# How entry 0's x is fetched at the start of a spectral filter with a SoLU block behind it: rows, transfers and queues

## The chip, the cores and the metric

The kernel runs on one core of a Trainium2 chip. The metric is the device time of one execution in microseconds (us); runs are summed up by their median. The engines are TensorE (PE; its weight loads are listed apart as PEld), VectorE (DVE), ScalarE (ACT), GpSimd (POOL) and SyncE (SP). SP, ScalarE and GpSimd can issue DMA transfers, each through a queue of its own; 16 DMA engines carry them.

## The reference

Eight entries of 3136 rows and 256 channels are filtered in the frequency domain along the rows; the 25088 rows that come out go through a block with two matrix products and a softmax-weighted activation between them. All is fp32.

```python
X = np.fft.rfft(x, axis=1)                     # x: 8 x 3136 x 256
y = np.fft.irfft(X * (filt_r + 1j * filt_i)[None], n=3136, axis=1)
h = y.reshape(25088, 256) @ w_in               # 256 x 1024
sm = softmax(h)
solu = h * sm
ln = (solu - mean(solu)) / sqrt(var(solu) + 1e-6) * g_ln
out = ln @ w_out                               # 1024 x 256
```

## The kernel before, in words

**The transform.** 3136 is 49 x 64 (`N1`, `N2`). A row number is 64 * n1 + n2. The kernel takes n2 together with 63 - n2: on the partitions, "half 0" holds the 49 values of n1 for n2 = 0 to 31 (partitions 0 to 48) and "half 1" the 49 values for n2 = 63 down to 32 (partitions 49 to 97), so half 1 is read mirrored, with a negative step. `rows_x` is the tile of entry 0: 98 partitions by 32 (`NH`) columns by 256 channels, a column being one value of n2. It is loaded in 8 pieces of 4 columns (`NCH`) for each half. In HBM, 4 columns of one n1 are 4 KB in a row, and the next n1 is 64 KB further.

**The opening**, entry 0, is in this order by engine:

- SP issues the table `wf_t` (L540), then half 0 of x (L535): piece 0 as 48 rows, then the 49th row of all 32 columns as one transfer of 32 KB, then pieces 1 to 7 as 48 rows each. After that come the stores of pa's last 4 rows.
- ScalarE's queue issues the table `one` (L541).
- GpSimd issues half 1 of x, 8 mirrored pieces of 49 rows (L535), with two blocks of `w_in` between them (`begin`, L425), then the tables and filter rows of the first four pairs of residues (`load_tables(0, 4)`, L481 and L484: one `de`, eight `f`), then those of the next four.
- TensorE runs `first` (L238, "pa") on each piece: two products of 98 x 100 by 98 x 512. ScalarE copies the result over x (L240) and stores it to the DRAM scratch `d1`: 96 rows from ScalarE's queue (L193), the other 4 from SP's (L194).
- TensorE then runs five products without use (`idle_row(5, "idle")`, L563), which read `de` and `f`, so they wait for all loads of `load_tables(0, 4)`.
- SP fetches `d1` back with frequencies on the partitions (`t`, then into spare places of `y`; L303). TensorE runs `forward` (L313, "pb"), VectorE and GpSimd multiply by the filter (L334 to L336), TensorE goes back (L313, "pc"), and ScalarE copies and stores `g` to the scratch `d2` (L351, L355).
- 14 more products without use ("idler", L563) stand before the last step of entry 0 (L409, "py"), which reads `d2` through SP's fetches (L363). SP then fetches half of entry 1's x (L476).
- Between these, VectorE, ScalarE and GpSimd turn the weights, which arrive as 64-bit numbers, into fp32 (`convert`).

**The rest.** From about 100 us on a loop over blocks of 128 rows (`step`) runs both matrix products, the activation and the transforms of the entries that follow; the changed code doesn't touch it.

The order of the work is written by hand (`tc.manual_schedule()`): each engine runs its instructions in the order in which the code emits them. The waits are derived from the tiles that are read and written. A DMA transfer tells of its landing by counting up a semaphore; there are eight such semaphores for the queues of SP and ScalarE together, used in turn, and eight for GpSimd's. The ninth transfer therefore takes the semaphore of the first, and where nothing else has ensured that the first has landed, the issuing engine waits for it.

## Time and profile before

| what | us |
|---|---|
| median of three runs | 1596.14 (1591.15 to 1606.48) |
| profiled execution | 1601.33 |
| its span | 1599.6 |
| TensorE's mean granted clock in it | 0.994 |

The profile is of one execution, so sums are made against its own 1601.33 us. The span runs from the first to the last instruction. The opening's other rows, from the timeline and the DMA view (queue, transfers, size of each):

| what | count and size |
|---|---|
| half 0 of x, SP | 8 of 192 KB and 1 of 32 KB |
| half 1 of x, GpSimd | 8 of 196 KB |
| raw blocks of `w_in` before the filters, GpSimd | 2 of 512 KB |
| `f` of the first eight pairs, GpSimd | 16 of 128 KB |
| stores of pa, ScalarE and SP | 8 of 384 KB and 8 of 16 KB |

pa's first product starts at 10.58 us and the last ends at 26.78; the eight copies of pa take 1.01 us each, the first at 14.35, the last at 28.07. The first filter product of VectorE (L334) starts at 43.30. How the profile is read: a line of the timeline or the chain gives a start and a length; an engine's "idle before" is put down to whatever released it last; and an idle engine off the chain costs nothing.

### The profile page before, as it was taken

What the parts mean: (1) busy time and instruction counts of PE and PEld (TensorE: products, weight loads), DVE (VectorE), ACT (ScalarE), POOL (GpSimd) and SP (SyncE); (2) the same over time, 40 slices, a digit from 0 to 9 for tenths busy, and PEclk for the clock granted to TensorE, in tenths of its full rate; (3) what the DMA queues carried; (4) which work ended last, traced back from release to release, by engine and by line L of the source; (5) the groups of instructions that cost most, each with busy time, mean ns of one, the idle gap of its engine ahead of it and who ended that gap; (6) DMA issues with size and microseconds to landing.
All of it is one profiled execution on the core that took longest, in us unless ns stands there. A gap on an engine that the chain in (4) does not pass through costs nothing.

```text
span 1599.6 us, 36769 instructions
## 1 busy us (share of the span) xinstructions
PE 1551.8 (97%) x12828; PEld 1058.8 (66%) x12828; DVE 1250.7 (78%) x2248; ACT 921.4 (58%) x1874; POOL 1169.7 (73%) x1371
## 2 busy tenths in 40 slices
PE   5998999999999999999999999999999999999997
PEld 1463566666666676677666677667766777777777
DVE  1887878897987788876988789887888777777673
ACT  2246555656665656666565655666565656666663
POOL 5546886789677868796779867797766766676765
PEclk8999999999999999999999999999999999999999
DMA  9989878786987589766886679766784444343434
GB/s 266 290 282 269 247 215 236 215 217 181 255 241 222 155 229 256 211 183 178 221 231 202 166 193 251 204 189 179 215 224 132 126 133 122 103 113 94 116 105 116
DMA packets 343802, 311.13 MB, mean 195 GB/s; under 512 B 27834, under 2 KB 310099, under 8 KB 343619
## 3 DMA queue, kind: packets, MB, share of 16 engines
q1 hardware_dynamic: 271476, 170.45, 40.6%
q0 software_dynamic: 33744, 98.81, 21.0%
q10 hardware_dynamic: 38400, 39.53, 8.2%
q8 instruction: 104, 1.70, 0.5%
q14 instruction: 78, 0.64, 0.1%
HBM read 124.51 MB, written 81.40 MB: 129 GB/s over the span
## 4 chain that ended last, share of the span: by engine, by line
PE 84%; DMA 9%; DVE 2%; POOL 1%; issue 1%; SPq 1%; ACT 0%; DVEq 0%; POOLq 0%; ACTq 0%
PE m L759 35%; PE o L895 34%; DMA solu_t<-turn 4%; PE py L386 4%; PE pc L313 3%; PE pb L313 3%; PE pa L281 2%; DMA x<-in_x_dram 2%; DMA f<-in_filt_r_dram 1%; SPq L840 1%; PE idler L563 1%; PE pa L238 1%; PE py L409 1%; DMA out_dram<-ot 1%; POOL u L738 1%
## 5 line engine op out<-in xcount | busy, mean ns | idle before, releaser
L895 PEld LDWEIGHTS o<-w_out_sb,solu_t 128*128 128x128 f32 x3136 | 381.5, 192 | 50.2 <-issue 43.6
L895 PE MATMUL o<-w_out_sb,solu_t 128*128 128x128 f32 x3136 | 400.9, 276 | 3.6 <-DVE ot L915 2.9
L759 PE MATMUL m<-w_in_sb,s 128*128 128x512 f32 x784 | 399.0, 610 | 2.7 <-ACT h L769 1.8
L895 PEld LDWEIGHTS o<-w_out_sb,u 128*128 128x128 f32 x2352 | 307.1, 192 | 138.9 <-issue 106.0
L895 PE MATMUL o<-w_out_sb,u 128*128 128x128 f32 x2352 | 310.6, 275 | 2.5 <-POOL u L738 1.8
L759 PE MATMUL m<-w_in_sb,y 128*128 128x512 f32 x588 | 307.6, 606 | 1.5 <-DVE h L780 1.1
L805 DVE SCALAR_TENSOR_TENSOR h<-e,h 128x1024 f32<-128x1024 f32 x196 | 304.1, 1551 | 0.1
L769 ACT COPY h<-m 128x512 f32<-128x512 f32 x294 | 173.2, 589 | 206.5 <-PE m L759 187.0
L911 ACT ACTIVATE ot<-o,rs_t 128x128 f32<-128x128 f32 x392 | 143.6, 368 | 245.2 <-PE o L895 243.8
L738 POOL TENSOR_TENSOR u<-solu_t 128x512 f32<-128x512 f32 x98 | 135.5, 1383 | 195.6 <-DMA solu_t<-turn 133.6
L783 DVE CUSTOM_DVE_ANT_0 h<-m,h 128x512 f32<-128x512 f32 x196 | 134.2, 685 | 176.8 <-ACT h L769 103.0
L813 ACT ACTIVATE h<-h,nmu 128x1024 f32<-128x1024 f32 x196 | 225.0, 1148 | 52.0 <-DVE turn L823 51.8
L823 DVE STREAM_TRANSPOSE turn<-h 128x1024 f32<-128x1024 f32 x196 | 243.1, 1240 | 3.2
L793 ACT ACTIVATE e<-h,nmax 128x1024 f32<-128x1024 f32 x196 | 225.4, 1150 | 7.9 <-DVE h L805 6.5
L738 POOL TENSOR_TENSOR u<-solu_t,u 128x512 f32<-128x512 f32 x98 | 137.7, 1405 | 95.8 <-PE o L895 95.5
L759 PEld LDWEIGHTS m<-w_in_sb,s 128*128 128x128 f32 x784 | 128.1, 191 | 89.5 <-issue 68.9
L915 DVE SCALAR_TENSOR_TENSOR ot<-o,rs_t,ot 128x128 f32<-128x128 f32 x299 | 103.7, 347 | 98.8 <-ACT ot L911 59.0
L738 POOL TENSOR_TENSOR u<-u,solu_t 128x512 f32<-128x512 f32 x98 | 159.1, 1624 | 15.5 <-PE o L895 6.4
L759 PEld LDWEIGHTS m<-w_in_sb,y 128*128 128x128 f32 x588 | 96.6, 191 | 96.7 <-issue 46.6
L738 POOL TENSOR_TENSOR solu_t<-solu_t,solu_t 128x512 f32<-128x512 f32 x98 | 153.9, 1571 | 0.9
L738 POOL TENSOR_TENSOR s<-y 128x128 f32<-128x128 f32 x196 | 99.8, 509 | 0.5
L386 PEld LDWEIGHTS py<-wb_t,t 50*64 50x64 f32 x3584 | 57.6, 134 | 42.9 <-issue 18.7
(126 smaller groups left out, 1969.1 us busy)
## 6 DMA issues: line engine op xcount, KB each, us to landing
solu_t<-turn SPq DMA_DIRECT2D x780, 128.0 KB
out_dram<-ot SPq DMA_DIRECT2D x196, 128.0 KB
t<-d POOLq DMA_DIRECT2D x112, 200.0 KB, 7.0
d<-x POOLq DMA_DIRECT2D x100, 200.0 KB, 5.3
f<-f_dram POOLq DMA_DIRECT2D x39, 512.0 KB, 8.1
t<-d ACTq DMA_DIRECT2D x37, 512.0 KB
d<-g POOLq DMA_DIRECT2D x36, 512.0 KB, 5.1
x<-in_x_dram SPq DMA_DIRECT2D x112, 98.0 KB
```

Source lines behind the costliest of these rows:

```text
L386: nc.tensor.matmul(out=views[g][64 * h:64 * h + 64, cb, i, :], lhsT=t4[rows, i, c0:c0 + 64], rhs=wb_t[rows, 0:N1], start=True, stop=True)
L738: nc.gpsimd.tensor_tensor(out=out, in0=in0, in1=in1, op=op)
L759: nc.tensor.matmul(out=ms[j, bank], lhsT=lhsT, rhs=w_in_sb[:, w, :], start=m in (1, 2, 7), stop=True, skip_group_check=True)
L769: nc.scalar.copy(out=h_half(k, i), in_=ms[j, 0])
L783: nc.vector.tensor_tensor_reduce(out=h_half(k, i), in0=ms[j, bank], in1=h_half(*kept), scale=1.0, scalar=sofar, op0=ALU.add, op1=ALU.min, ...
L793: nc.scalar.activation(out=e, in_=hs[k], func=AFT.Exp, bias=nmaxs.pop(k)[:, 1:2], scale=-1.0, accum_out=esums[g][:, i:i + 1])
L805: nc.vector.scalar_tensor_tensor(out=solu, in0=e, scalar=SHRINK, in1=solu, op0=ALU.mult, op1=ALU.mult, accum_out=nmu)
L813: nc.scalar.activation(out=solu, in_=solu, func=AFT.Square, bias=nmu, scale=-float(DFF), accum_out=variances[g][:, i:i + 1])
L823: nc.vector.transpose(out=turns[g][:, :, i, :], in_=solus[k].rearrange("p (f j) -> p f j", j=32))
L895: nc.tensor.matmul(out=pos[p, bank], lhsT=lhs[:, f, :], rhs=w[:, f, :], start=f == 0 and (m in (1, 2, 7) or alone), stop=True, skip_group_ ...
L911: nc.scalar.activation(out=out_half(p, *to)[0], in_=pos[p, 0], func=AFT.Copy, scale=rs)
L915: nc.vector.scalar_tensor_tensor(out=ot, in0=pos[p, bank], scalar=rs, in1=out_half(p, *kept)[0], op0=ALU.mult, op1=ALU.add)
```

## The change

Both halves of x are fetched as 48 rows for a piece. The two 49th rows (one of each half) come in four transfers, each with every second column, 16 columns of 1 KB: two from SP, two from ScalarE's queue. The first mirrored piece is issued by ScalarE in place of GpSimd; the other seven stay with GpSimd. In the changed file the lines after L538 stand 8 to 10 further on.

```diff
+        def fetch_last_rows(h, odd, dma):
+
+            row, first = N1 * h + N1 - 1, odd if h == 0 else N2 - NH + 1 - odd
+            places = slice(odd, NH, 2) if h == 0 else slice(NH - 2 + odd, None, -2)
+            dma(out=rows_x[row:row + 1, places],
+                in_=bass.AP(tensor=x.tensor, offset=x[0].offset + ((N1 - 1) * N2 + first) * C,
+                            ap=[[N2 * C, 1], [2 * C, NH // 2], [1, C]]))
+
         st.enter_context(tc.manual_schedule())
         nc.sync.dma_start(out=wf_t, in_=wf_dram)
         nc.scalar.dma_start(out=one, in_=one_dram)
         pieces = NH // NCH
 
         fetch_x(0, 0, NCH, 0, N1 - 1, nc.sync.dma_start)
-        fetch_x(0, 0, NH, N1 - 1, 1, nc.sync.dma_start)
-        for i in range(pieces):
-            if i:
-                fetch_x(0, NCH * i, NCH, 0, N1 - 1, nc.sync.dma_start)
-            fetch_x(1, NCH * i, NCH, 0, N1, nc.gpsimd.dma_start)
+        fetch_x(1, 0, NCH, 0, N1 - 1, nc.scalar.dma_start)
+        for odd in range(2):
+            for h in range(2):
+                fetch_last_rows(h, odd, (nc.sync, nc.scalar)[h].dma_start)
+        for i in range(1, pieces):
+            fetch_x(0, NCH * i, NCH, 0, N1 - 1, nc.sync.dma_start)
+            fetch_x(1, NCH * i, NCH, 0, N1 - 1, nc.gpsimd.dma_start)
             if i in (4, 7):
                 begin(i // 7)
         load_tables(0, 4, nc.gpsimd.dma_start)
```

`fetch_x(h, n0, n, r0, rows, dma)` loads `rows` rows from row `r0` on and `n` columns from `n0` on of half `h`.

Compared with before, the program's instructions on VectorE and TensorE are the same; in the opening SP issues one transfer more, ScalarE three more and GpSimd one fewer; from pa's stores on, the order on every engine is the one of before.

## The prediction

> **What bounds the kernel now.** I read the page first, to see how large the opening is against the rest; then the chain of waits in order of time over the first 150 us; then the waits and the timeline of the opening; then busy times by stretches of 5 us.

> The page's header, its first table and its chain by engine:

> ```profile
> span 1599.6 us, 36769 instructions
> PE 1551.8 (97%) x12828; PEld 1058.8 (66%) x12828; DVE 1250.7 (78%) x2248; ACT 921.4 (58%) x1874; POOL 1169.7 (73%) x1371
> PE 84%; DMA 9%; DVE 2%; POOL 1%; issue 1%; SPq 1%; ACT 0%; DVEq 0%; POOLq 0%; ACTq 0%
> ```

> TensorE is busy 97% of the span, so 47.8 us without a matmul are all that exists outside its work, and the change touches only the first loads. The chain in order of time (start, length, what) shows what the loads gate:

> ```profile
> 3.15 12.68 DMA x<-in_x_dram
> ...
> 16.87 12.21 DMA f<-in_filt_r_dram
> ...
> 30.26 4.98 DMA f<-in_filt_r_dram
> 35.24 2.04 PE idle L563 x2
> ...
> 42.15 1.04 PE pb L313 x16
> ...
> 69.39 12.21 PE idler L563 x28
> 81.61 11.31 PE py L409 x102
> 92.92 8.22 DMA y<-in_x_dram
> ```

> The reader should see that TensorE's first transform (pa) is not on the chain at all: x loads, then GpSimd's filter loads, then the five idle products, then pb. From pb on, the chain is mostly TensorE work in a fixed order, so what reaches pb's start reaches the end unless a later transfer is not moved with it. The timeline (start, length, engine, line, what, idle before it and its releaser) gives the places:

> ```profile
> 1.22 5.43 SPq L535 DMA_DIRECT2D x<-in_x_dram  x9
> 1.38 3.98 POOL L535 DMA_DIRECT2D x<-in_x_dram  x5 [0.93 <-POOLq L1161]
> 10.58 16.19 PE L238 MATMUL pa<-x,wf_t 98*100 98x512 f32 x32 [10.58 <-DMA x<-in_x_dram]
> 10.82 0.74 POOL L535 DMA_DIRECT2D x<-in_x_dram  x1 [3.38 <-DMA x<-in_x_dram]
> 35.23 6.93 PE L563 MATMUL idle<-f,de 128*128 128x512 f32 x10 [8.45 <-DMA f<-in_filt_r_dram]
> 36.56 0.40 SPq L303 DMA_DIRECT2D t<-d  x1
> 42.08 0.66 PEld L313 LDWEIGHTS pb<-t,de 64*64 64x64 f32 x16 [0.76 <-PE idle L563]
> ```

> TensorE waits twice: 10.58 us for the first x, 8.45 us for the filters. pb is released by the idle products (42.08), not by t. The stretches of 5 us (stretch, length, busy time and count of PE, PEld, DVE, ACT, POOL, then clock, DMA share, GB/s) show that transfers fill the opening:

> ```profile
> 5.00:10.00 5.00, 0.00 (x0) 0.00 (x0) 0.00 (x0) 0.00 (x0) 2.44 (x4) 1.00 1.04 222
> 15.00:20.00 5.00, 5.00 (x13) 2.03 (x12) 0.00 (x0) 2.45 (x4) 1.88 (x3) 1.00 1.03 213
> 25.00:30.00 5.00, 1.77 (x5) 0.40 (x3) 3.07 (x7) 2.25 (x3) 2.08 (x4) 0.87 1.03 415
> 30.00:35.00 5.00, 0.00 (x0) 0.00 (x0) 0.69 (x1) 0.99 (x2) 3.58 (x7) 0.50 0.96 321
> ```

> The last column but one is the DMA share: about 1 throughout. The bytes before pb do not change, so a new order alone buys nothing; what can be bought is uneven loading of the 16 DMA engines. The completion counts that the trace keeps (16 for a transfer) show it. The first mirrored piece has 15 counts by 6.97 us and the last at 10.54; the later mirrored pieces end 12.34, 15.83, 16.57 and so on to 24.23, the last count 0.8 to 2.8 us behind the fifteenth; the filter loads after them inherit it (29.08 against 26.01). One DMA engine is some 3 us in arrears until about 33 us. Where this comes from: the 49th row of half 0 is one packet of 32 KB, on one engine, started at 3.85 and 1.93 us long; a 4 KB packet of x takes 0.28 to 0.31 us on average. The other suspect is 49 rows over 16 engines, at least 4 packets somewhere against 3 for 48 rows: 0.3 us more for a piece, 2.4 us over eight.

> **The change, part by part.**

> *The 32 KB row goes (SP issues one fewer), four transfers of 16 columns come, two from SP, two from ScalarE.* Issue costs 0.27 to 0.47 us each in SP's x rows and 0.31 to 0.38 in ScalarE's. On ScalarE three issues (the moved piece's too) make 1.1 us, done by 2.3 us; its next work is the table load at 10.59. Without that cover they would cost 1.1 us. On SP one more issue is 0.3 us ahead of pieces 1 to 7, hidden below. If the 16 columns go to 16 DMA engines, each carries 1 KB a transfer, 4 KB in all: 0.05 us a packet by the 1 KB packets of t (46 ns), so 0.2 us against the 1.93 us packet. By the rows shown, a transfer uses a number of engines that divides its rows: 98 rows 14, 96 rows 16, 49 rows 7, 4 rows 4, the one row 1 (the rest of the 16 counts come at issue: 15 at 2.18, the last at 6.32). Read by rows alone the new transfers would sit on one engine, 64 KB of it, 3.9 us at 1.93 for 32 KB, worse than before. I take 16, as the pattern that the instruction carries is 1 x 16 x 256 and its first size above one is 16. [...]

> *Three small transfers more.* Each occupies its queue for its issue only: SP's first pieces are issued 0.3 to 0.5 us apart while earlier ones are in flight, and land at most 2.9 us apart. Cost on the path 0, bounds 0 and 0.6 us (the slowest small landing behind piece 0). [...]

> *The first mirrored piece goes from GpSimd to ScalarE's queue, with 48 rows, and the other seven become 48.* GpSimd saves one issue of 0.75 to 1.0 us; its eighth x issue no longer waits 3.38 us; its next issues, the second raw block and de, still wait for pieces 1 and 2. The first matmul then waits for piece 0 of half 0 (landed 4.92), the mirrored piece (fifteenth count 6.97 while it ran on GpSimd's queue) and the small rows. I put it at 6.5, bounds 5.5 and 10.6: 4.1 us earlier. None of that is on the path by itself; it moves the copies and stores of pa.

> *A new wait.* In the changed order each transfer of SP and ScalarE waits for the one eight before it. So SP's pieces 1 to 4, free before (issued 2.04 to 3.32), now wait for the two tables (2.6 to 2.8), then piece 0 of each half (about 5 and 6); pieces 5 to 7 for the small rows. Behind them on SP stand only the 4-row stores, which need copies from 14.35 on. Their readers are pa 1 to 7. Pieces 1 and 2 with the rest of piece 0 are 9 packets an engine, 2.6 us at 0.29 alone and more with two queues beside them, which covers the 2.1 us between 2.8 and 4.9. Cost 0; uncovered, up to 1 us on pa 3.

> *The end of x.* The last mirrored piece goes from 24.23 to its fifteenth count, 21.43, or a little earlier: pa ends near 24.0 in place of 26.78. Between 10.58 and 15 us matmuls run at about half speed (0.85 us apart, then 0.43); starting early, that happens while pieces are still arriving, so it costs nothing.

> *pb's two gates.* First the filters: the last of entry 0's eight loads was issued at 28.28, on a count of 27.99 whose fifteenth was 25.21, and landed 34.92, fifteenth 34.01. So it gains between 0.9 (own laggard) and 2.8 us (issue too); one transfer fewer ahead (196 KB, 0.9 us at 222 GB/s) supports the upper half: 2.0. The idle products take 6.93 us because the granted clock is 0.5 until 38.97; if that moment stays, half of what is gained before it is lost, if it moves along nothing is: 1.0 to 2.0, I take 1.5. Second t: the last store landed 36.54, fifteenth count 34.56, its fetch was issued 36.56 and t landed 41.31, 0.8 us before it was needed. It gains 2.0 with 0.8 of slack, so it does not take over. pb starts at 40.6.

> *After pb.* The 14 idler products (12.2 us), py and the second entry's x follow on TensorE; SP's t fetches (74.74 on), which wait for the last g store (74.99), move with pb. The first t4 piece lands 78.43, 3.0 us ahead of py at 81.44. I pass the 1.5 us through whole.

> Sum: profiled execution 1601.33 (span 1599.6 and 1.7 around it) - 1.5 = 1599.8. That execution lies 5.2 above the median 1596.14 of the three runs; on the median, **1594.6**.

> **Rivals.**

> 1. *Filters later, slower.* The stores of pa (400 KB each) start about 4 us sooner and compete with the filter loads between 10 and 30 us. In 25 to 30 us, with stores, 415 GB/s were moved, but by the packet records GpSimd's queue had only 113 to 145 of it, against 230 alone (14 to 18 us). Three stores moved ahead of the filters are 1.2 MB, 2.9 us at 415. It decides once the last filter lands after 34.92; net of the 1 to 2 us won, 1 to 2.5 us slower: 1598. For: DMA share near 1. Against: loads and stores move more bytes together than loads alone, and the issue of the filters is paced by the x pieces.
> 2. *It doesn't do what it says:* the four small transfers use one engine each, the same one. The arrears stay, pa's start is near 8, pb's at 42 to 43: 1596.5.
> 3. *More than forecast:* filters and stores both gain the full 3 us and the clock rises with them, plus 1 us from fewer uneven packets: 4 us, 1592.

> **How the numbers follow.** Forecast 0.58, filters later 0.18, one engine 0.14, more 0.10. All are under 0.3% of the time, so the range is made by the scatter: the runs shown reach from 1591.15 to 1606.48, 0.96%, which is why 1% is about what a measurement here can tell from no change. Low end 1591.15 - 4 = 1587; high end the profiled 1601.33 + 2.5 = 1604. Only scatter could put it beyond 1%: 0.04 on either side, 0.92 between.

> **What would show it.** Right: first pa matmul at 5.5 to 8 us; the mirrored pieces' last counts within 1 us of their fifteenth; pa's end near 24; idle products from 33; pb near 40.6; py near 80; all later work the same length. Wrong: new small rows landing after 8 us (rival 2), the idle products starting after 35.2 although pa starts early (rival 1), or pb's gain gone by py.

## The result and the profile after

| | before | after |
|---|---|---|
| median, us (20 runs each, side by side) | 1600.03 (1589.99 to 1607.03) | 1593.63 (1588.38 to 1601.52) |
| profiled execution, us | 1601.33 | 1593.74 |
| its span | 1599.6 | 1592.0 |

The ratio is 0.9963 with a 95% interval of 0.9945 to 0.9982: 5.9 us faster, at least 2.9 and at most 8.8. Before's median in this comparison is 3.9 us above that of its first three runs, so the ratio, not the medians' distance from the forecast, is what counts.

Page of after, header and first table:

```profile
span 1592.0 us, 36774 instructions
PE 1549.7 (97%) x12828; PEld 1060.1 (67%) x12828; DVE 1249.5 (78%) x2248; ACT 921.2 (58%) x1874; POOL 1169.2 (73%) x1370
```

TensorE's busy time fell by 2.1 us and its time without a matmul from 47.8 to 42.3. The opening of after is read from its timeline (start, length, engine, line, what, idle before it and its releaser; L543 issues the small rows, the four new transfers of 16 columns):

```profile
1.72 1.54 ACTq L543 DMA_DIRECT2D x<-in_x_dram  x2
1.73 1.26 SPq L543 DMA_DIRECT2D x<-in_x_dram  x2
...
9.01 17.22 PE L238 MATMUL pa<-x,wf_t 98*100 98x512 f32 x32 [9.01 <-DMA x<-in_x_dram]
...
27.62 0.31 ACTq L193 DMA_DIRECT2D d<-x  x1
...
28.99 6.77 PE L573 MATMUL idle<-f,de 128*128 128x512 f32 x10 [2.77 <-DMA f<-in_filt_i_dram]
...
35.25 0.40 SPq L303 DMA_DIRECT2D t<-d  x1
...
39.08 1.69 PE L313 MATMUL pb<-t,de 64*64 64x256 f32 x16 [3.32 <-DMA t<-d]
40.70 2.08 PE L497 MATMUL back<-one,de 128*128 128x128 f32 x8
42.71 1.17 PE L313 MATMUL pb<-y,de 64*64 64x256 f32 x16
```

The filters release the idle products at 28.99 in place of 35.23, 6.2 us earlier. pb starts only 3.0 earlier (39.08 against 42.08): t now comes last. pb waits 3.3 us for it, where before pb followed the idle products at once. pb works in units, each on one fetched tile (t, then y): a line "pb ... x16" is one unit. Its second unit starts 3.63 us after the first; before they were 2.14 apart (42.08, 44.22). The stretches say why (stretch, length, busy time and count of PE, PEld, DVE, ACT, POOL, granted clock, DMA share, GB/s):

```profile
35.00:38.00 3.00, 0.76 (x2) 0.00 (x0) 0.00 (x0) 0.00 (x0) 1.82 (x2) 1.00 0.45 126
38.00:41.00 3.00, 1.92 (x17) 1.14 (x18) 0.19 (x1) 0.00 (x0) 0.00 (x0) 0.75 1.09 384
41.00:44.00 3.00, 3.00 (x25) 2.27 (x25) 2.97 (x5) 0.59 (x1) 0.00 (x0) 0.68 1.11 371
```

TensorE stood idle from 35.8 to 39.1, and the granted clock is 0.5 from 39.5 to 42.9, just when pb runs. 1.5 us (3.63 less 2.14) of what was gained goes there; in two more executions of the changed kernel these two units were 2.9 and 3.94 apart, 1.4 us lost on the mean of the three. From the first unit to the fourth it is 8.83, 8.88 and 10.17 us, against 7.28 in each of three profiles of before: 2.0 us lost on the mean.

Single executions differ, so before and the changed kernel were each profiled three times (experiments below). Means of the three, in us:

| | before | changed | gain |
|---|---|---|---|
| pb starts | 42.8 | 39.0 | 3.8 |
| py starts | 82.3 | 80.1 | 2.1 |
| first product of the main loop (`ps_mean`) | 105.2 | 103.7 | 1.5 |
| from there to TensorE's last product | 1483.9 (1477.8 to 1490.1) | 1482.6 (1482.4 to 1482.9) | 1.3, inside the scatter |

The 1.7 us that go missing between pb and py fit the 2.0 lost over pb's first units. The next 0.6 is one profile's: from py to `ps_mean` after took 24.78 us, with the clock at 0.5 from 100.93 to 104.34, and in the five other profiles 22.8 to 23.0.

### The profile page after: what moved, and what is told of

It is laid out like the page before. It is cut to its first block, busy times and chain, and to the rows that moved or that the text cites. A ratio compares the mean times of both kernels' runs of the same rounds, so it can differ in the third digit from the quotient of the medians.

```text
span 1592.0 us, 36774 instructions
## 1 busy us (share of the span) xinstructions
PE 1549.7 (97%) x12828; PEld 1060.1 (67%) x12828; DVE 1249.5 (78%) x2248; ACT 921.2 (58%) x1874; POOL 1169.2 (73%) x1370
## 4 chain that ended last, share of the span: by engine, by line
PE 59%; DMA 2%; issue 0%; POOL 0%; SPq 0%; DVE 0%; POOLq 0%; DVEq 0%
PE o L905 27%; PE m L769 26%; PE py L386 2%; PE pc L313 1%; PE pb L313 1%; PE pa L281 1%; DMA solu_t<-turn 1%; DMA x<-in_x_dram 0%; DMA de<-de_tbl 0%; SPq L850 0%; PE o L869 0%; POOL u L748 0%; POOL x L272 0%; POOL solu_t L748 0%; DVE turn L833 0%
```

## Experiments

Going in, two theories stood for the uneven DMA engines: the 32 KB row on one engine, as the prediction had it (R), or the 49 rows of the mirrored pieces (N). The third question was whether the queue of the first mirrored piece matters (Q). Ratios are against before on the same chip.

**e1_row: before, with only the 32 KB row split in two.**

```diff
-        fetch_x(0, 0, NH, N1 - 1, 1, nc.sync.dma_start)
+        for odd in range(2):
+            fetch_last_rows(0, odd, nc.sync.dma_start)
```

> The kernel before with one part of the change: the 32 KB row becomes two transfers of 16 columns from SP; half 1 stays as it was. Theory R (the one 32 KB packet puts one DMA engine in arrears): the mirrored pieces' last counts come under 1 us behind their fifteenth, first pa between 7 and 9 us, the last of entry 0's eight filter loads at 29 to 31 us in place of 34.9, time 2 to 4 us under before. Theory N (49 rows over 16 engines do it): the last counts stay 2 to 3 us behind, the last filter lands at 34 or later, time as before. Theory Q (the moved first piece and GpSimd's shorter queue do it): as before in all.

**e2_back32: the changed kernel, with the 32 KB row back in one transfer.**

```diff
-        for odd in range(2):
-            for h in range(2):
-                fetch_last_rows(h, odd, (nc.sync, nc.scalar)[h].dma_start)
+        fetch_x(0, 0, NH, N1 - 1, 1, nc.sync.dma_start)
+        for odd in range(2):
+            fetch_last_rows(1, odd, nc.scalar.dma_start)
```

> The changed kernel with the 49th row of half 0 again as one transfer of 32 KB from SP. R: last counts again 2 us behind the fifteenth, the last filter load at 31 us or later in place of 28.8, time 1 to 3 us over the changed kernel. N and Q: no arrears, the last filter within 0.7 us of 28.8, time as the changed kernel.

**e3_stay: the changed kernel, with the first mirrored piece (48 rows) back on GpSimd.**

```diff
-        fetch_x(1, 0, NCH, 0, N1 - 1, nc.scalar.dma_start)
+        fetch_x(1, 0, NCH, 0, N1 - 1, nc.gpsimd.dma_start)
```

> The changed kernel with the first mirrored piece, 48 rows, back at the head of GpSimd's queue. Q: the last filter load 2 us or more later than the changed kernel's 28.8, the eighth x issue of GpSimd waits again, time 2 to 4 us over the changed kernel. R and N: at most 0.9 us later (one transfer of 192 KB more ahead of the filters), time within 1 us of the changed kernel.

**e4_48: both of the last edits**, which is before with 48 rows for the mirrored pieces and half 1's 49th row apart (two transfers from ScalarE's queue), and nothing else.

```diff
-            fetch_x(1, NCH * i, NCH, 0, N1, nc.gpsimd.dma_start)
+            fetch_x(1, NCH * i, NCH, 0, N1 - 1, nc.gpsimd.dma_start)
...
+        for odd in range(2):
+            fetch_last_rows(1, odd, nc.scalar.dma_start)
```

> The kernel before with one part of the change: half 1 in pieces of 48 rows, its 49th row in two transfers of 16 columns from ScalarE's queue; the 32 KB row and GpSimd's first piece stay. N: last counts under 1 us behind the fifteenth, the last filter at 29 to 32 us. R: arrears of some 2 us stay, the last filter at 32 to 34 us (0.3 us a piece gained), time 0 to 2 us under before. Q: as before.

What the profiles show of the opening, one profile each ("behind" is the last completion count behind the fifteenth, over the mirrored pieces on GpSimd's queue):

| | 32 KB row | mirrored rows | first piece from | last mirrored piece | behind | last filter | pb | ratio |
|---|---|---|---|---|---|---|---|---|
| before | yes | 49 | GpSimd | 24.23 | 0.8 to 3.6 | 34.92 | 42.08 | 1 |
| e1_row | no | 49 | GpSimd | 24.57 | 0.1 to 1.3 | 34.83 | 42.06 | 0.9995 (0.998 to 1.0011) |
| e4_48 | yes | 48 | GpSimd | 20.86 | 0.1 to 0.9 | 31.92 | 38.88 | 1.0 (0.9979 to 1.0021) |
| e3_stay | no | 48 | GpSimd | 19.18 | up to 0.5 | 29.65 | 37.61 | 1.0003 (0.998 to 1.0025) |
| e2_back32 | yes | 48 | ScalarE | 20.96 | 2.1 to 4.0 | 31.15 | 40.32 | 0.9994 (0.9974 to 1.0015) |
| after | no | 48 | ScalarE | 18.18 | up to 0.3 | 28.80 | 39.08 | 0.9963 (0.9945 to 0.9982) |

Down the column of the last filter: 48 rows for 49 bring 5.2 us without the 32 KB row (34.83 to 29.65) and 3.0 with it (34.92 to 31.92). The 32 KB row costs 2.3 and 2.35 with 48 rows, and 0.1 with 49. The queue brings 0.85, which can't be told from scatter: in three profiles each the last filter landed at 34.92, 35.07 and 35.53 before and at 28.80, 29.13 and 27.89 in the changed kernel. So the forecast that the split row alone moves the filters missed: e1 takes the arrears away, and the last filter stays at 34.83, and TensorE's wait too (its timeline):

```profile
35.13 7.00 PE L572 MATMUL idle<-f,de 128*128 128x512 f32 x10 [6.81 <-DMA f<-in_filt_r_dram]
42.06 1.11 PE L313 MATMUL pb<-t,de 64*64 64x256 f32 x16
```

What 49 rows do is in the DMA view over the first 45 us: GpSimd's queue (packets, MB, share of 16 engines), then its mirrored pieces (count, KB each, median us from issue to landing). Before, then e4_48:

```profile
q0 software_dynamic: 2240, 5.29, 46.2%
...
x<-in_x_dram POOLq DMA_DIRECT2D x8, 196.0 KB, 13.1
```

```profile
q0 software_dynamic: 1728, 5.24, 39.3%
...
x<-in_x_dram POOLq DMA_DIRECT2D x8, 192.0 KB, 9.5
```

Eight rows fewer should be eight packets fewer, and they are 512. The other 504 are packets of 16 bytes; the packet records have them in before and e1_row, and none where all mirrored pieces have 48 rows. 504 is 63 for a piece, 9 times 7, which I read as 7 rows of a piece on each of 7 engines, and on each of the other nine as many packets that carry next to nothing. The records don't name the engine of a packet, so the 7 by 7 is read from these counts and from before's 49-row transfers on SP's queue (entry 1's x, from 85.61 us on), which count up once at their issue (86.09) and 7 times as they land (91.56 to 93.18). The 48-row pieces of half 0 count up 16 times (piece 0: 3.34 to 4.92), read as 3 rows on each of 16. By this reading the engines that carry data have 28 KB of a piece to move in place of 12. The small packets themselves are not the cost: all 504 took 6.7 us of engine time in before, some 0.4 us if it is spread over 16 engines.

The medians of e1 to e4 were 1594.45, 1594.37, 1596.5 and 1597.96, against 1596.82 for before: in the times, none of the four differs from before. For e1 that agrees with its pb. For e2 a gain of 2.5 us (its pb against the mean of before's three) lies inside the interval, which ends at 4.1. e3 is the surprise: pb 4.5 us before that of before and no gain. Its profile, an execution of 1604.13 us, shows where it can go. The waits of TensorE after 36 us (us in total, times, longest us):

```profile
PE pb L313 <- DMA y<-d: 7.0, 1, 7.0
```

SP's timeline in e3:

```profile
39.58 8.14 SPq L484 DMA_DIRECT2D f<-in_filt_i_dram  x4
48.29 0.38 SPq L303 DMA_DIRECT2D y<-d  x1
```

and the stretches in which that falls:

```profile
50.00:53.00 3.00, 0.41 (x4) 0.21 (x2) 2.12 (x4) 0.75 (x2) 1.60 (x3) 0.93 0.96 309
53.00:56.00 3.00, 0.00 (x0) 0.00 (x0) 0.00 (x0) 0.00 (x0) 1.82 (x3) 0.50 1.06 393
56.00:59.00 3.00, 1.57 (x16) 0.95 (x16) 0.00 (x0) 0.00 (x0) 0.00 (x0) 0.50 0.92 355
59.00:62.00 3.00, 3.00 (x15) 0.97 (x14) 0.00 (x0) 0.00 (x0) 0.00 (x0) 0.50 0.07 30
```

pb's fifth unit waits 7.0 us for its rows, which SP fetches only after its eight filter loads, which semaphores hold up; GpSimd's fetches of the units behind it go out at 47.15, ahead of SP's at 48.29. TensorE is idle in 53 to 56 us, and its clock stays at 0.5 until 62.8. Some 10 us go there in this execution, which is 7.6 us above e3's median, so not every run loses as much: the idler products start at 74.44, later than before's 69.32. In e1, e2 and e9 (below) the same unit waits 0.8 to 1.9 us, in one of three profiles of before 0.3, in after and e4 not at all.

e4 stays unexplained: pb at 38.88, py at 78.21, the earliest but one of all, and yet the median is that of before. Its interval ends at a gain of 3.4 us, its pb came 3.2 (by the pair) to 3.9 (by before's three) earlier. Its profiled execution, 1600.17, lost the lead after the opening: its main loop began at 101.16 us, 4.0 before the mean of before's three, and took 1492.0 us, where before's took 1477.8 to 1490.1.

**e5_same: the changed kernel once more**, beside the next three.

> The changed kernel once more, beside the runs of the kernel before. Theory P (what moves the start of pb moves the end by as much): 2 to 4 us under before, ratio 0.9975 to 0.9988. Theory S (the 6 us of the first comparison were partly scatter, and what pb gains is lost again before 110 us): ratio 0.998 to 1.000. If the first figure holds as it is: 0.995 to 0.997.

Measured 1593.11 against 1598.81: 0.9968 (0.995 to 0.9985), 5.1 us. The first figure repeats, a larger gain than P and S had. Its pb starts at 39.26, after a wait of 2.8 us for t.

**e6_delay: the changed kernel with 14 idle products more before pb**, which moves pb and nothing else ahead of it. It asks whether what reaches pb reaches the end.

```diff
-        idle_row(5, "idle")
+        idle_row(19, "idle")
```

> The changed kernel with 19 idle products ahead of pb in place of 5, 14 more at 0.86 us. pb starts at 47 to 48.5 us in place of 39.1. P: the end is 8 to 9 us later than the changed kernel's, about 1602 where that has 1593.5. A (a later transfer, the fetch of unit 4 or what follows it, is the gate, and pb has slack): less than 5 us later.

Measured 1601.86, 1.0012 (0.9992 to 1.0032): 8.75 us over e5_same by the medians, 7.0 by the two ratios. Its timeline:

```profile
48.06 1.11 PE L313 MATMUL pb<-t,de 64*64 64x256 f32 x16
...
50.19 1.11 PE L313 MATMUL pb<-y,de 64*64 64x256 f32 x16
```

pb starts 8.8 us later than in e5_same and py 7.4 later (87.38 against 79.98): TensorE doesn't idle before pb here, the units are 2.13 apart, and that gives some of the delay back. What reaches py arrives at the end, as far as the intervals tell; a later gate that would have hidden the delay (A) is out.

**e7_fetch4: the changed kernel, with SP's fetch of the unit that made e3 wait put ahead of the eight filter loads; e8_both: the same on e3_stay.**

```diff
-        def load_tables(i0, n, dma):
+        def load_tables(i0, n, dma, between=lambda: None):
...
+            between()
...
-        for i in range(1, units - 2):
+        for i in range(1, 4):
...
-            if i == 3:
-                load_tables(8, NP - 8, nc.sync.dma_start)
+        load_tables(8, NP - 8, nc.sync.dma_start,
+                    lambda: sp.fetch(4, nc.sync.dma_start, spare_piece(3)))
```

> The changed kernel with the fetch of unit 4 issued by SP before the eight filter loads of the last pairs instead of after them. Theory L (that fetch is the next gate, and where it lands late TensorE stalls and its clock is halved): it is issued near 38 us in place of 46, pb's fifth unit waits for nothing, the idler row starts at 67.6 or earlier, no run above 1600, time 1 to 3 us under the changed kernel. Otherwise: as the changed kernel, within 1 us.

> The same reordering with the first mirrored piece, 48 rows, at the head of GpSimd's queue (the kernel e3_stay with unit 4's fetch first). L: pb at 37 to 38 us, no stall of TensorE before its fifth unit (7.0 us in e3_stay), idler row at 64 to 66 us in place of 74.4, time 3 to 5 us under before. Otherwise: as e3_stay, within 1 us of before.

Measured 1592.5, 0.9958 (0.9938 to 0.9977), and 1591.94, 0.9959 (0.9942 to 0.9975). SP's timeline in e8:

```profile
36.45 1.79 SPq L303 DMA_DIRECT2D y<-d  x1
38.28 2.75 SPq L485 DMA_DIRECT2D f<-in_filt_r_dram  x4
```

The fetch goes out at 36.45 and pb waits for none of its units. On e3 this makes a kernel that showed no gain over before into one that is 6.6 us (0.41%) faster than before, and the intervals of the two ratios (0.998 to 1.0025, 0.9942 to 0.9975) don't meet, so the late fetch was where e3's gain went. On the changed kernel, which showed no such wait, it is worth 0.6 us by the medians (1592.5 against 1593.11), less than the runs resolve. Both are faster than before; that either is faster than the changed kernel is not shown.

**f1_before, f2_before, f3_after: before twice more and the changed kernel once, one profiled execution each.** They ask where the rest of the 5 us lies: in half-clock stretches of the opening (G), or in the main loop (H).

> The kernel before once more, for a second profile. Theory G (half of the gain is clock that the opening loses in the kernel before): pb near 42 us, 10 us at half clock between 25 and 45 us as in the first profile, against 6.8 to 10.2 in the changed kernel's two. Theory H (the clock differs in the loop, not in the opening): half-clock windows after 110 us, two in the first profile, again at least two, against one and none in the changed kernel's.

> The same a third time. G and H as for the second profile; if pb lies away from 42 us by more than 1.5 us in either, the first profile's opening was not typical and the 3.0 us gained by pb have to be taken from the means.

> The changed kernel a third time. pb at 39 to 39.5 us, released by t, the filters landed near 29 us; no stall of TensorE before pb's fifth unit. G: under 7 us at half clock between 25 and 45 us; H: at most one half-clock window between 110 and 1500 us.

The times were 1590.65, 1596.71 and 1593.38, 1592.04 for before beside them. The starts of pb, 43.19, 43.14 and 38.68, repeat those of the first pair; the timeline of f2_before has the old order, filters last and pb at once behind the idle products:

```profile
35.83 7.38 PE L563 MATMUL idle<-f,de 128*128 128x512 f32 x10 [6.73 <-DMA f<-in_filt_r_dram]
43.14 1.11 PE L313 MATMUL pb<-t,de 64*64 64x256 f32 x16
```

G fell: between 25 and 45 us the half clock lasted 10.2, 10.2 and 6.8 us in before's three profiles, and 6.8, 10.2 and 10.2 in those of the changed kernel. H isn't shown: between 110 and 1500 us there were 2, 0 and 0 stretches of half clock before and 1, 0 and 1 in the changed kernel, and the loop took 1490.1, 1477.8 and 1483.9 us before, 1482.4 to 1482.9 changed, and the scatter of before alone is larger than what is looked for.

**e9_idle9: the changed kernel with four idle products more**, so that TensorE isn't idle while t is on its way (theory K: the idle window costs the half clock at pb).

```diff
-        idle_row(5, "idle")
+        idle_row(9, "idle")
```

> The changed kernel with 9 idle products ahead of pb in place of 5: they fill the 3 to 4 us for which TensorE waits for t. Theory K (that wait halves the clock for pb's first units, and so eats 1 to 1.7 of the 3.8 us gained at pb): full clock from pb on, pb's second unit 2.1 us after the first in place of 2.9 to 3.9, pb at 39 to 40 and py at 78.2 to 79.5 in place of 79.8 to 80.7; time 1 us under the changed kernel, which the comparison can hardly tell. Otherwise: py at 80 or later, as the idle products only move pb.

Its timeline, then its stretches over pb:

```profile
29.49 11.13 PE L573 MATMUL idle<-f,de 128*128 128x512 f32 x18 [3.61 <-ACT raw L456]
40.55 1.11 PE L313 MATMUL pb<-t,de 64*64 64x256 f32 x16
...
42.68 1.11 PE L313 MATMUL pb<-y,de 64*64 64x256 f32 x16
```

```profile
38.00:41.00 3.00, 3.00 (x15) 1.23 (x17) 0.00 (x0) 0.00 (x0) 0.00 (x0) 1.00 1.01 344
41.00:44.00 3.00, 3.00 (x39) 2.00 (x31) 2.21 (x4) 0.59 (x1) 0.00 (x0) 1.00 1.05 342
```

The clock is whole and pb's units are 2.13 apart again, so K holds for the clock. The rest of it doesn't: pb starts at 40.55, 1.5 us later than in the changed kernel (39.0), which is about what the whole clock saves, and py at 83.50 in place of the 78.2 to 79.5 expected, as in this profile pb's fifth unit waits 1.9 us and the clock is at 0.5 from 55.48 to 58.9. The time, 1593.29 against 1599.1, 0.997 (0.9949 to 0.9991), is as the changed kernel had.

## Why the prediction was right, and where not

The forecast was 1.5 us less, and within 1%; 5.9 and 5.1 were measured. The direction and the place were right, several sizes were not, and two errors worked against each other; that pb's start came within 1.5 us of the forecast (39.08 against 40.6) is luck.

- *Sixteen columns on sixteen engines:* right, as far as the counts tell. Each of the four small rows has 16 counts (SP's first from 4.98 to 6.50), where before's 32 KB row has one at its issue (2.18) and one at its landing (6.32). No transfer of before's opening has 16 columns for its first size, so until the changed kernel ran the 16 was the author's reading of the pattern. Rival 2, one engine each, is out, although the sign that was named for it, a small row landing after 8 us, did come (8.77, next point).
- *Three small transfers at no cost, bounds 0 and 0.6:* wrong. ScalarE's second small row lands at 8.77, behind piece 0 of each half (4.65 and 5.33), and that releases the first matmul at 9.01, not at 6.5. In e1, e3 and e4, whose ScalarE queue carries no piece of x, it starts at 6.97 to 7.37; in e2, where it carries the piece and two small rows as here, at 9.98. The filters don't wait for pa, so they lost nothing by this; but pa's stores set t (below).
- *"Starting early, it costs nothing":* wrong. pa's products are 0.85 us apart until 14.96 before and until 15.07 after, then 0.43; the moment of full speed did not move with pa's start, so after has more of the slow ones, and of 1.6 us gained at pa's start 0.6 is left at its end, 26.22, where 24.0 was forecast. *The new wait of SP's pieces at no cost* was right: TensorE waits for x once, 9.0 us.
- *The arrears:* half right. The 32 KB row does cost time: with 48 rows the filters come 2.3 us later by it (e3 against e4, after against e2), close to the 2.0 forecast. But taken away alone it brings 0.1 (e1), and the late last counts that were to show it come and go without the cost: e4 and e2 both have the row, and are 0.1 to 0.9 and 2.1 to 4.0 us behind.
- *"49 rows over 16 engines, at least 4 packets somewhere against 3":* this is the term that was mis-sized, at 0.3 us a piece and 2.4 over eight, of which only rival 3 counted 1 us. By the counts above the packets are 7 against 3 on those engines. Four packets more at 0.28 us would be 1.1 a piece if the same engines took every piece; from e1 to e3 the last mirrored piece moves 5.4 us, 0.67 a piece. By rows alone the prediction itself had 49 rows on 7 engines, in its passage on the small transfers, and didn't carry it over to the mirrored pieces.
- *The filters gain 2.0 (0.9 to 2.8):* 6.1, from 34.92 to 28.80, for both reasons together.
- *"It gains 2.0 with 0.8 of slack, so it does not take over":* the gain was about right and the conclusion wrong, which kept the error small. t landed 2.4 us earlier (41.31 to 38.94), 1.3 of it by its issue (36.56 to 35.25): ScalarE's last store, held by a store four before it, went from 29.36 to 27.62 only. But with filters 6 us early, t is last, and pb gains 3.0 in the pair.
- *The idle products' half clock, 1.0 to 2.0 lost or kept:* it came in another place. The idle products hardly changed (6.93 to 6.77); the 3.3 us of waiting for t bring half the clock over pb, 1.4 us by its second unit and 2.0 by its fourth, on the mean of three.
- *Passed through whole:* nearly right for a later pb, 7.0 to 8.75 of 8.8 us in e6. Of an earlier pb it isn't shown: in the changed kernel 2.1 of 3.8 us are left at py, and behind pb e3's fetch of the fifth unit was last.
- *Rival 1* (filters later) is refuted by 34.92 to 28.80. *Rival 3* (4 us) comes closest in size, with 1 us for the uneven packets where they made most of the filters' gain.

What stays open: pb comes 3.8 us earlier by three profiles each, which lies inside both intervals (2.9 to 8.8 and 2.4 to 8.0); but only 2.1 of it is left at py and 1.5 at the loop's start, and the other 3.6 to 4.4 of the measured 5.1 and 5.9 have no place in any profile. In e5's twelve runs the mean granted clock is 0.9958, against 0.9941 in the runs of before beside it; times 1594 and 1599 us, that is 6.7 us lost to the clock against 9.4, so 2.7 us go with the clock there. In the twenty runs of the first comparison the changed kernel's mean is 0.9949 (before's isn't on record there), which against the same 0.9941 would leave 1.3. Where in the loop the clock differs wasn't found. Nor is it explained why e4, with pb as early as the changed kernel's, shows no gain; so it is not shown that the earlier pb makes the measured time.

## What to carry to other kernels

Count the engines that a transfer uses before counting its bytes: one row less for a piece, with the odd rows apart, brought the last filter forward by 3.0 to 5.2 us here, the 32 KB packet that looked like the laggard by 0.1 to 2.35. In the kernel's time neither alone showed a gain. When a load is made earlier, look at once at what comes second, and by how little: here a slack of 0.8 us became a wait of 3.3 us and a stretch of half clock. A fetch queued behind loads that wait on semaphores (SP's, behind eight filter loads) was on time in the profiles of after and e4 and held TensorE for 7.0 us in that of e3; put it ahead of them.
